# A two-head kernel rewritten: folded filter, three real products, taps on TensorE, transposing loads, one written-out order

## The chip, the cores and the metric

The kernel runs on one core of a Trainium2 chip. The core has a matrix engine (TensorE, PE in the profile, with its weight loads as PEld), a vector engine (VectorE, DVE), a scalar engine (ScalarE, ACT), a general engine (GpSimd, POOL) and a queue engine (SyncE, SP); the engines run side by side, each through its own instructions in order, and wait for one another by semaphores. DMA transfers are issued from the queues of SP, ACT and POOL. The time is the device time of one execution in microseconds.

## The reference

Two independent heads work on 2048 positions of 576 channels, in bf16, and their outputs stand side by side.

```python
def _A_ref(x, wqkv, wo):                     # H = 32 heads of 18 channels, W = 8 taps, dil = 2
    qkv = (x @ wqkv) ...                     # q, k, v
    idx = pos[:, None] - off[None, :]        # positions s, s-2, ..., s-14
    logits = jnp.einsum("bhsd,bhswd->bhsw", q, kg) * scale
    attn = _softmax(jnp.where(mask, logits, -1e9))
    o = jnp.einsum("bhsw,bhswd->bhsd", attn, vg)
    return o... @ wo

def _B_ref(q, k, v, shift_k, ssm_k, ssm_D):
    k_shift = sum over t < 4 of k_pad[:, t:t+S] * shift_k[:, 3-t]
    kv = k_shift * v
    y = irfft(rfft(kv, padded) * rfft(ssm_k, padded))[:S]     # a causal convolution of length 2048
    y = y + kv * ssm_D
    return q * y
```

Head A is an attention in which each position sees eight earlier positions two apart. Head B multiplies a short filter of k with v, convolves the product with a long filter per channel, adds a skip term and gates with q.

## The kernel before

Positions are cut into four blocks of 512 (`NBL`, `BL`), and head A also into two halves of 1024 (`hh`, `jj`).

Head B. The loads of k and v bring positions onto the partitions. `taps` (L412) forms the four-tap filter and the product with v on VectorE: per block four multiplications (L417), three additions (L420) and one multiplication by v (L421), each of 2304 elements. `mirror` (L423) turns half a block around on TensorE (L430) and adds and subtracts it by DMA, so that a transform of 256 rows per sign is enough for the data. `filter_spectrum` (L457) multiplies each block of 512 filter taps, loaded by transposing DMA into `kTok`, with cosine and sine tables `TK`: per block eight units of four pairs of matmuls (`mm3`, L454 and L455, 384 and 192 columns), each evicted by ScalarE (L466) into `Ks`. `turn_filter` (L474) adds neighbouring blocks of the filter's spectra by six DMAs on POOL's queue, three links of two. `x_spectrum` (L513) does the same for the data into `xw`, two pairs of matmuls a unit. `products` (L753) multiplies a data spectrum with a filter spectrum as complex numbers, four real products of 768 elements in one VectorE instruction (L757), 30 of them; `sums` (L764) adds them in PSUM with identity matrices in 64 x 64 tiles (L777); `inverse` (L789) goes back to positions (L799, L802), mirrors (`back`, L810), and the inner `gate` multiplies with q (L820) and stores.

Head A. x is partly turned on TensorE (L356, L370), partly loaded by transposing DMA (`turn_x`, L163). `project` (L276) makes q, k and v, with the 64 last rows of the contraction paired in two row groups (L297). `logits` (L541) multiplies q with shifted k on VectorE (L550) and sums over the channels of a head on TensorE (L559). `softmax` (L568) runs on VectorE and ScalarE. `spread` (L619) copies attention weights over partitions by DMA (L626), `weigh` (L638) multiplies them with v (L648) and adds over the eight taps in PSUM (L664, L675), and `output` (L696) multiplies with `wo` (L702, L705) and stores.

The order: VectorE's work is written in a fixed sequence. TensorE's units that can be moved (projections, spectra, inverses, outputs) stand in a list `units`; `until` (L252) takes a number of them, written out in `PLACES`, between the fixed steps. PSUM is two pools of two double banks. SP carries most loads, in the order in which the program issues them.

Of the kernel before, what the change touches and what calls it, by code (L numbers as in the profile page):

```python
# [18 lines left out]
PLACES = (  # L19
    11, 10, 11, 15, 1, 1, 2, 1, 1, 3, 0, 3, 2, 0, 3, 5, 2, 0, 4, 3, 4, 2, 1, 3, 1, 0, 6, 1, 7, 4, 4, 4, 2, 5,  # L20
    3, 2, 3, 0, 1, 2, 1, 2, 0, 1, 0, 2, 1, 0, 0, 0, 1, 2, 0, 1, 0, 1, 1, 2, 0, 1, 2, 3, 0, 0, 2, 1,
)


def view(t, offset, dims):

    return bass.AP(tensor=t.tensor, offset=t.offset + offset, ap=[list(t.ap[0])] + [list(d) for d in dims])
# [3 lines left out]
def kernel(  # L31
# [24 lines left out]

    PAD = 16
    KW = PAD + S
    KWH = PAD + 1024

    NBL, BL = 4, 512


    GORD = [0, 2, 1, 3]
    HD = 288
    SPB = 2 * 4 * D
    TH = 192

    ctx.enter_context(tc.manual_schedule())
    main = ctx.enter_context(tc.tile_pool(name="main", bufs=1))
    pp = ctx.enter_context(tc.tile_pool(name="pp", bufs=2, space=PSUM))

    def bank2(name, tag):
        return pp.tile([128, 2, 512], FP32, name=name, tag=tag)

    XW = 2 * SPB
    xw = main.tile([128, 4 * SPB], BF16, name="xw")  # L90
    TK = main.tile([128, 4, 2, BL], BF16, name="TK", tag="tabk")
    TX = main.tile([128, 2, 2, BL], BF16, name="TX", tag="tabx")
    TI = main.tile([128, 4, 2, 256], BF16, name="TI")

    def xT(kb, t0, n):
        return view(xw, XW + SPB * (t0 // 1024) + 1024 * kb + t0 % 1024, [[1, n]])

    def x5(jj):
        return view(xw, XW + SPB * jj + 4096, [[1, 512]])

    def wq(kb, comp, c0, n):
        return view(xw, comp * 5 * D + kb * D + c0, [[1, n]])


    wv = view(xw, 0, [[5 * D, 3], [D, 5], [1, D]])

    def load_w(eng, comp, to=None):
        to = wv[:, comp] if to is None else to
        eng.dma_start(to[:, 0:4, :], A_wqkv[0:512, comp * D:(comp + 1) * D].rearrange("(kb p) a -> p kb a", p=128))
        for r in range(2):  # L110
            eng.dma_start(to[64 * r:64 * r + 64, 4, :], A_wqkv[512:576, comp * D:(comp + 1) * D])

    s1 = ExitStack()
    sp1 = s1.enter_context(tc.tile_pool(name="s1", bufs=1, reuse_waits="tile"))
    pib = main.tile([128, 1], FP32, name="pib")
    nc.vector.memset(pib[:], float(np.float32(np.pi)))
    onesb = main.tile([1, 128], BF16, name="onesb")
    nc.vector.memset(onesb[:], 1.0)
    warm = sp1.tile([128, 1], FP32, name="warm")
    nc.scalar.activation(warm[:], pib[:], ACT.Sin)  # L120
    skrow = sp1.tile([1, 4 * D], BF16, name="skrow", tag="wraw")
    nc.sync.dma_start(skrow[:], B_shift_k.rearrange("d j -> (d j)").unsqueeze(0))

    Ks = main.tile([128, NBL, 2, 3, 4, TH], BF16, name="Ks")
    xnat = view(Ks, 0, [[4 * D, 4], [D, 4], [1, D]])
    n_all = view(Ks, 16 * D, [[1, 16 * D]]).bitcast(I32).rearrange("p (n f) -> p n f", n=9)
    krs = [view(Ks, 2 * D * i, [[D, 2], [1, D]]) for i in range(NBL)]
    kTok = main.tile([128, NBL, 4, D], BF16, name="kTok", tag="r_ktok")
    kjs, vts = [], []

    def load_x(qtr):
        nc.sync.dma_start(xnat[:, qtr], xf[512 * qtr:512 * qtr + 512, :].rearrange("(sb p) c -> p sb c", p=128))

    load_x(0)
    load_x(1)

    def load_k(i):

        eng = nc.sync
        kj = sp1.tile([128, 7, D], BF16, name="kj", bufs=2)  # L140
        r0 = BL * i
        if i == 0:
            nc.vector.memset(kj[0:1, 0:3, :], 0.0)
            eng.dma_start(kj[:, 3:7, :], kf[0:BL, :].rearrange("(p c) d -> p c d", c=4))
            for p0, p1 in ((1, 113), (113, 128)):
                eng.dma_start(kj[p0:p1, 0:3, :], bass.AP(tensor=kf.tensor, offset=kf.offset + (4 * p0 - 3) * D,
                                                         ap=[[4 * D, p1 - p0], [D, 3], [1, D]]))
        else:
            eng.dma_start(kj[:], bass.AP(tensor=kf.tensor, offset=kf.offset + (r0 - 3) * D,
                                         ap=[[4 * D, 128], [D, 7], [1, D]]))  # L150
        kjs.append(kj)

    def load_v(i):
        vt = sp1.tile([128, 4, D], BF16, name="vt", bufs=2)
        nc.sync.dma_start(vt[:], vf[BL * i:BL * i + BL, :].rearrange("(p c) d -> p c d", c=4))
        vts.append(vt)

    def load_filter(m):

        nc.sync.dma_start_transpose(kTok[:, m, :, :], B_ssm_k[:, BL * m:BL * m + BL])  # L160

    load_w(nc.sync, 0)
    def turn_x(h):  # L163

        r0 = 1024 + 512 * h
        nc.sync.dma_start(xnat[:, 2 + h, :, 512:576], xf[r0:r0 + 512, 512:576].rearrange("(sb p) c -> p sb c", p=128))
        nc.sync.dma_start_transpose(view(xw, XW + SPB + 512 * h, [[1024, 4], [1, 512]]), xf[r0:r0 + 512, 0:512])

# [312 lines left out]
    for i in range(NBL):  # L481
# [19 lines left out]
        if i == 2:  # L501
            load_filter(3)
# [396 lines left out]
```

## Time and profile before

| | |
|---|---|
| median of 3 runs | 238.58 us (237.65 to 240.54) |
| span of the profiled execution | 239.0 us |
| granted TensorE clock, mean | 0.984 |
| instructions | 4802 |
| bytes moved by DMA | 33.75 MB in 29559 packets |

The span of the profiled execution agrees with the median of the runs within 0.2%. In the rows of the profile, "L757" is a line of the kernel; "out<-in" names what an instruction writes and reads; after the bar stand the busy time of the group, the mean duration of one in ns, and the idle time of its engine just before. A matmul's duration includes the time until its results are out, so matmuls that follow one another overlap, and the distance between starts is the price of one in a row of them.

### The profile page before, as it was taken

To read this page: it belongs to the slowest core of one execution; us is meant where nothing else is said; L and a number is where in the kernel's file an instruction comes from. 1 tells how busy PE (TensorE), PEld (TensorE's weight loads), DVE (VectorE), ACT (ScalarE), POOL (GpSimd) and SP (SyncE) were. 2 spreads that over 40 slices of the span, in tenths; PEclk is the share of its full clock that TensorE was granted. 3 is DMA by queue.
4 is the path that set the end of the run, shared out by engine and by line. 5 is a ranking of instruction groups with operands and counts; after the bars stand their busy time and mean duration, and the time that the engine had idled before them with its cause. 6 is when DMAs were issued, how large, how long until landed. Compare 5 with 4: busy or idle time off the path is not lost.

```text
span 239.0 us, 4802 instructions
## 1 busy us (share of the span) xinstructions
PE 219.5 (92%) x2032; PEld 116.5 (49%) x2041; DVE 206.0 (86%) x152; ACT 156.7 (66%) x213; POOL 28.9 (12%) x61
## 2 busy tenths in 40 slices
PE   4899998999899999999998976989999999999991
PEld 2533443345545566533343443445555666666550
DVE  7599999999898896989899593889997899999931
ACT  6796778579965568565585575454568766736551
POOL 8600010202120000402108100000000000000000
PEclk9999999999999999999999999799999999999996
DMA  6999999999541000299975999907203102323233
GB/s 198 309 224 326 247 289 148 352 154 199 105 81 22 0 0 3 38 164 225 188 137 99 129 265 251 265 21 247 76 27 101 51 3 101 99 101 101 99 103 99
DMA packets 29559, 33.75 MB, mean 141 GB/s; under 512 B 16577, under 2 KB 23617, under 8 KB 29537
## 3 DMA queue, kind: packets, MB, share of 16 engines
q1 hardware_dynamic: 23712, 22.08, 38.0%
q0 software_dynamic: 3648, 9.00, 19.1%
q10 hardware_dynamic: 2176, 2.36, 2.9%
q8 instruction: 16, 0.26, 0.5%
q14 instruction: 7, 0.05, 0.1%
HBM read 13.11 MB, written 4.72 MB: 75 GB/s over the span
## 4 chain that ended last, share of the span: by engine, by line
PE 58%; DVE 21%; ACT 9%; SPq 5%; DMA 3%; issue 2%; DVEq 0%
PE ps_z L777 9%; PE ps_fk L454 8%; PE ps_wo L702 7%; PE ps_inv L799 7%; PE ps_proj L284 6%; SPq L626 5%; PE ps_log L559 4%; PE ps_fk L455 4%; DVE ab L420 3%; DVE tB L417 3%; PE ps_acc L664 3%; DMA X<-attn 3%; PE ps_acc L675 2%; DVE qk L648 2%; PE ps_back L810 2%
## 5 line engine op out<-in xcount | busy, mean ns | idle before, releaser
L757 DVE TENSOR_TENSOR qk<-xw,Ks 128x3072 bf16<-128x3072 bf16 x30 | 50.7, 1752 | 2.2 <-PE ps_z L777 2.0
L284 PE MATMUL ps_proj<-xw 128*128 128x512 bf16 x183 | 47.4, 385 | 2.2 <-ACT v L306 1.0
L550 DVE TENSOR_TENSOR prod<-qk 128x4096 bf16<-128x4096 bf16 (+1 forms) x20 | 40.6, 2074 | 4.3 <-PE ps_log L559 3.9
L454 PE MATMUL ps_fk<-kTok,TK 128*128 128x384 bf16 x128 | 32.6, 327 | 0.4 <-ACT qk L306 0.2
L455 PE MATMUL ps_fk<-kTok,TK 128*128 128x192 bf16 x128 | 31.4, 246 | 0.0
L284 PEld LDWEIGHTS <-xw 128*128 128x128 bf16 x192 | 17.1, 99 | 23.4 <-issue 8.6
L466 ACT ACTIVATE Ks<-ps_fk 128x576 bf16<-128x576 f32 x32 | 20.6, 651 | 12.0 <-PE ps_fk L455 11.9
L518 ACT ACTIVATE xw<-ps_fx 128x576 bf16<-128x576 f32 x32 | 19.9, 649 | 7.5 <-PE ps_fx L455 7.3
L306 ACT ACTIVATE qk<-ps_proj 128x1024 bf16<-128x1024 f32 x18 | 18.6, 1035 | 8.7 <-PE ps_proj L297 8.5
L784 ACT ACTIVATE Yall<-ps_z 128x768 bf16<-128x768 f32 x24 | 18.1, 810 | 4.4 <-PE ps_z L777 4.4
L454 PE MATMUL ps_fx<-ab,TX 128*128 128x384 bf16 x64 | 18.2, 332 | 1.8 <-ACT xw L518 1.7
L799 PE MATMUL ps_inv<-Yall,TI 128*128 128x288 bf16 (+2 forms) x128 | 19.0, 287 | 0.6 <-ACT yA L811 0.6
L702 PE MATMUL ps_wo<-qk,pv 128*128 128x288 bf16 x128 | 18.4, 287 | 0.6 <-ACT xw L518 0.6
L454 PEld LDWEIGHTS <-TK 128*128 128x128 bf16 x128 | 12.5, 98 | 12.4 <-issue 5.0
L803 ACT ACTIVATE yA<-ps_inv 128x576 bf16<-128x576 f32 (+2 forms) x16 | 10.4, 652 | 10.9 <-PE ps_inv L802 7.1
L777 PE MATMUL ps_z<-qk,ident 64*64 64x384 bf16 x288 | 16.7, 326 | 0.0
L420 DVE TENSOR_TENSOR ab<-ab,tB 128x2304 bf16<-128x2304 bf16 x12 | 16.3, 1358 | 0.4
L417 DVE TENSOR_TENSOR tB<-kj,skb 128x2304 bf16<-128x2304 bf16 x12 | 16.3, 1356 | 0.3
L648 DVE TENSOR_TENSOR P<-X,v 128x4096 bf16<-128x4096 bf16 x6 | 13.6, 2288 | 2.7 <-DMA X<-attn 1.2
L664 PE MATMUL ps_acc<-P,ident 64*64 64x512 bf16 x192 | 15.7, 379 | 0.3 <-DVE P L648 0.3
L455 PE MATMUL ps_fx<-ab,TX 128*128 128x192 bf16 x64 | 15.8, 247 | 0.0
L799 PEld LDWEIGHTS <-TI 128*128 128x128 bf16 x128 | 11.4, 98 | 6.8 <-issue 3.8
(126 smaller groups left out, 349.0 us busy)
## 6 DMA issues: line engine op xcount, KB each, us to landing
Ks<-Ks POOLq DMA_DIRECT2D x6, 576.0 KB, 11.5
qk<-attn SPq DMA_DIRECT2D x12, 256.0 KB, 7.0
kj<-in_B_k_dram SPq DMA_DIRECT2D x3, 1008.0 KB, 6.4
vt<-in_B_v_dram SPq DMA_DIRECT2D x4, 576.0 KB, 6.0
qB<-in_B_q_dram POOLq DMA_DIRECT2D x4, 576.0 KB, 4.1
out_dram<-qk ACTq DMA_DIRECT2D x8, 288.0 KB, 2.4
X<-attn SPq DMA_DIRECT2D x8, 256.0 KB, 9.4
out_dram<-qB SPq DMA_DIRECT2D x3, 576.0 KB, 4.8
```

The source lines that it names most:

```text
L284: nc.tensor.matmul(ps[:, jp, :], wq(kb, comp, 128 * ct, 128), xT(kb, 1024 * jj + 512 * jp, 512), start=(kb == 0), stop=False)
L417: dve(2304, lambda: nc.vector.tensor_tensor(o, kj[:, 3 - j:7 - j, :], skb[:, j, :].unsqueeze(1).to_broadcast([128, 4, D]), ALU.mult))
L420: dve(2304, lambda: nc.vector.tensor_tensor(kv, kv, o, ALU.add))
L454: nc.tensor.matmul(o[:, 0:2, :], w, rhs[:, 0:2, :], start=start, stop=stop)
L455: nc.tensor.matmul(o[:, 2, :], w, rhs[:, 2, :], start=start, stop=stop)
L466: nc.scalar.activation(Ks[:, 3 - m, cs, :, gi, :], acc3(ps), ACT.Copy, scale=(CSG, SSG)[cs][m] * 2.0 / 1024.0)
L550: r = dve(1024 * nj, lambda: nc.vector.tensor_tensor(view(prod, 0, [[256 * nj, 4], [256, nj], [1, 256]]), view(t, o + 256 * hh, [[0, 4], [ ...
L664: nc.tensor.matmul(acc[64 * o:64 * o + 64, h, :], ident[64 * h:64 * h + 64, 64 * h:64 * h + 64], view(P, 256 * u, [[2048, 2], [1, 256]])[6 ...
L702: nc.tensor.matmul(ps[:, r, 0:HD], oT(hh, j + 2 * r, t)[:, o:o + 128], wo[:, t // 2, t % 2, HD * h:HD * h + HD], start=(t == 0), stop=False)
L757: r = dve(3072, lambda: nc.vector.tensor_tensor(pr, view(xw, i * SPB + 4 * TH * t, [[4 * D, 2], [0, 2], [1, 4 * TH]]), view(Ks, (3 - j + i ...
L777: nc.tensor.matmul(acc[r][o:o + 64, h, 0:2 * TH], w[64 * h:64 * h + 64, 64 * h:64 * h + 64], pr[64 * h:64 * h + 64, part, cs, 2 * TH * s:2 ...
L799: nc.tensor.matmul(ps[:, c, 0:n], TI[:, sl, pm, 128 * c:128 * c + 128], Yall[:, j % 2, pm, sl, c0:c0 + n], start=(sl == 0), stop=(pm == 0 ...
```

## The change

The program is rewritten; most functions have new bodies. What differs:

- **Order.** All steps are first put into a list of 685 operations by name; a string `ORDER` then says in which order they are emitted and which PSUM slot (one of four double banks, or a pair of two) an operation takes. `PLACES` and its bookkeeping go. All SBUF buffers but some small ones are regions of one tile `mem`.
- **Loads.** Three quarters of x, all of k and v and all of the filter come through transposing DMA on SP's queue, so that channels lie on the partitions; the second quarter of x is loaded plainly (`xn`) and turned on TensorE (`nx0` to `nx2`). The weights are issued from ACT's queue. k and v are loaded in two parts of 1024 positions (`k0`, `va0`, `vb0`, ...; `k1`, ...), the second into the same buffers after the first. In the queue, the order is x, then parts of k, v and the filter mixed: `xt0 x0 x2 hl1 xt2 kt0 va0 hl0 vat0 k0 xt3 x3 hu1 hm0 hl3 vb0 hu0 vbt0 hl2 hu2 hu3`, then `vbt1 vat1 k1 hm1 vb1 ho1 kt1 va1`.
- **Taps.** The four-tap filter is done on TensorE, with diagonal matrices of `shift_k` in 64 x 64 tiles; VectorE multiplies the result in PSUM with v, the lower half of each block read backwards. `fold` turns and folds the product with matmuls against `[I | -I]` and `[I | I]`.
- **Filter.** Each block of 512 taps is folded at its middle tap into an even and an odd part of 256, by DMA: the lower half goes to a scratch in DRAM, is copied there in reverse order (`hm0`, `hm1`) and added by accumulating DMAs. Spectra take two pairs of matmuls a unit instead of four. They are written over the memory of x and the weights, so they start after the v projections. `turn_filter` adds neighbouring blocks with 18 DMAs of a third each.
- **Products.** A complex product is three real ones: besides the two parts of a spectrum their sum (`S`) or difference (`W`) is kept, one VectorE instruction each per block, and `products` multiplies three planes for one or two blocks at a time (2304 or 4608 elements). `sums` adds them with 32 x 32 tiles at all 16 places of the array.
- **Attention sums.** `weigh` adds four channel groups in one unit, also in 32 x 32 tiles. The projection of v picks strided columns of the weights and writes 64 columns per matmul; the tail of the contraction is padded with zeros to a fifth full block.
- **Inverse and gates.** The inverse works on thirds of 192 channels. The sum and the difference of its two parts are taken on VectorE. For three blocks the lower half of the output is left in mirrored order, gated with a mirrored q (`qm`, a copy in DRAM), stored to a scratch (`y0l` to `y2l`) and copied in reverse order to the output (`y0m` to `y2m`); for the last block TensorE flips it.

VectorE's order from the first logits on is: logits of the first half, taps of the first half of k and v mixed with the first softmax, logits of the second half, second softmax mixed with the second taps, the 18 products of `weigh`, the sums `W` and `S`, the products `z` with the gates. TensorE's order begins (names: `p` component, channel tile, half; `L` logit sums; `t` taps; `f` fold; `k` filter spectra; `x` data spectra; `a` attention sums; `Z` sums; `i` inverse; `o` output):

```
nx1 nx0 nx2 p000 p010 p110 p100 p120 p020 L000 L001 p130 p030 L010 L011 p200 L012 L002 p140 p040 L003
p240 p141 p111 p121 p001 L013 L014 L004 t00 t01 t04 p210 p230 t03 t02 p101 p011 f000 p021 p031 L110 f010
L100 f011 p131 L111 L101 p041 p201 L102 p241 p211 L112 L103 p231 L113 f001 k200 L104 L114 k220 p221 k100
k300 f02 t14 t10 t11 f12 ...
```

The core of the diff (added lines; `mm`, `act`, `tt` are matmul, activation and tensor_tensor, `M` and `M1` views of `mem`):

```diff
+def emit(op, slot, PS):
+    if op.take:
+        a, b = (slot, slot + 1) if op.take == 1 else PAIRS[slot]
+        op.box.ps, op.box.step = PS[:, 2 * a:2 * a + 2], 1024 * (b - a)
+    op.fn()
...
+    VS, US = AB - 18432, AB - 9216
...
+    def load_x(qtr):
+        xbar(f"x{qtr}", M(XT + 512 * qtr, [[2048, 4], [1, 512]]), xf[512 * qtr:512 * qtr + 512, 0:512])
+        xbar(f"xt{qtr}", M1(X4 + 512 * qtr, 512), xf[512 * qtr:512 * qtr + 512, 448:576])
+
+    def load_k(pr):
+        c0, r0, r1 = (PAD, 0, 1024) if pr == 0 else (0, 1008, 2048)
+        xbar(f"k{pr}", M(KT + c0, [[1040, 4], [1, r1 - r0]]), kf[r0:r1, 0:512])
+        xbar(f"kt{pr}", M1(KT + 4 * 1040 + c0, r1 - r0), kf[r0:r1, 448:576])
...
+    def taps(pr):
...
+            def unit(box=box, jobs=jobs):
+                for l in range(4):
+                    for w, h, ab, c, bank in jobs:
+                        mm(box.ps[64 * c:64 * c + 64, bank, :], dg(w, h, l), kt(w, h, ab, l), start=(l == 0),
+                           stop=(l == 3), tile_position=(64 * h, 64 * c))
...
+            for lo in range(2):
+                s = [[512, nb], [1 - 2 * lo, 256]]
+                b = 255 if lo else 256
+                op(f"t{pr}{n}{'hl'[lo]}", lambda box=box, s=s, b=b, lo=lo, n=n, nb=nb: tt(
+                    M(KV + 1024 * n + 256 * lo, [[512, nb], [1, 256]]), view(box.ps, b, s), M(VT + 1024 * n + b, s),
+                    ALU.mult), box, free=bool(lo))
...
+                dma(f"hm{d // 2}", low_rows(scm, (d - 1) * 256, [[256 * D, 2], [D, 255], [1, D]]),
+                    low_rows(scr, (d - 1) * 256 + 255, [[256 * D, 2], [-D, 255], [1, D]]))
...
+    def filter_spectrum(m, cs, gi):
...
+            for c in range(2):
+                mm3(box.ps, M1(TK + 1024 * c + 512 * cs + 128 * gi, 128), thirds((HO if cs else HU) + 2 * D * m + D * c),
+                    c == 0, c == 1)
...
+    def turn_filter(m):
+        for t in range(3):
+            for cs, (x, y) in enumerate(((US, VS), (VS, US))):
+                dma(f"turn{m}{cs}{t}", M1(x + SPB * (3 - m) + 768 * t, 768), M1(y + SPB * (4 - m) + 768 * t, 768),
+                    nc.gpsimd, accum_op=ALU.add)
...
+                for u in range(W):
+                    for s in range(4):
+                        for i in range(4):
+                            o = i ^ s
+                            mm(view(box.ps[32 * o:32 * o + 32], box.step * (i // 2) + 512 * (i % 2), [[1, 512]]), I32S[1][32 * i:32 * i + 32],
+                               M(Ps[s] + 256 * u, [[2048, 2], [1, 256]])[32 * i:32 * i + 32],
+                               start=(u == 0), stop=(u == W - 1), tile_position=(32 * i, 32 * o))
...
+        op(f"z{j}{t}{i}", lambda: tt(
+            M(pr, [[2304, n], [768, 3], [1, 768]]), M(BS + i * SPB + o, [[SPB, n], [PL, 3], [1, 768]]),
+            M(VS + (3 - j + i) * SPB + o, [[SPB, n], [PL, 3], [1, 768]]), ALU.mult))
...
+            for k, (src, st, n, o, w) in enumerate(terms):
+                for g in range(4):
+                    for r in range(4):
+                        c = r ^ g
+                        mm(view(box.ps[32 * c:32 * c + 32], box.step * (r // 2) + 512 * (r % 2) + o, [[TH, n], [1, TH]]),
+                           I32S[w][32 * r:32 * r + 32], M(pr + src + TH * g, [[st, n], [1, TH]])[32 * r:32 * r + 32],
+                           start=(i == 0 and k == 0), stop=(i == j and k == len(terms) - 1),
+                           tile_position=(32 * r, 32 * c))
...
+        op(f"g{j}h", lambda: tt(M1(y + 2304, 1152), M1(y, 1152), M1(y + 1152, 1152), ALU.subtract))
+        op(f"g{j}l", lambda: tt(M1(y, 1152), M1(y, 1152), M1(y + 1152, 1152), ALU.add))
+        g = M(qb, [[1152, 2], [1, 1152]])
+        op(f"g{j}g", lambda: tt(g, M(y, [[2304, 2], [1, 1152]]), g, ALU.mult))
...
+        dma(f"y{j}m", rows(outf, (BL * j + 255) * 2 * D + D, [[HD, 2], [-2 * D, 256], [1, HD]]),
+            rows(scy[:], o, [[HD, 2], [D, 256], [1, HD]]))
```

More of the change, by code (lines that the diff above doesn't have):

```diff
@@ L1 @@
-from collections import deque
 from contextlib import ExitStack
-from functools import partial
 import numpy as np
@@ L105 @@
[L105 to L125, printed above, removed]
```

1245 lines of the change are left out of this document (610 added, 635 removed).

## The prediction

> **What bounds the kernel now.** I read the first part of the page, then the busy time by stretches of 12 us, then the groups by line with the shapes apart, then the timeline of TensorE and of the DMA queues for the price of single steps.
>
> ```profile
> PE 219.5 (92%) x2032; PEld 116.5 (49%) x2041; DVE 206.0 (86%) x152; ACT 156.7 (66%) x213; POOL 28.9 (12%) x61
> PE 58%; DVE 21%; ACT 9%; SPq 5%; DMA 3%; issue 2%; DVEq 0%
> ...
> 0.00:12.00 12.00, 7.95 (x48) 4.68 (x49) 7.51 (x18) 8.67 (x13) 8.66 (x35) 1.00 0.83 254
> 144.00:156.00 12.00, 9.30 (x73) 4.55 (x72) 7.98 (x4) 5.79 (x10) 0.00 (x0) 0.86 0.98 249
> 192.00:204.00 12.00, 12.00 (x170) 8.04 (x166) 11.88 (x8) 7.83 (x12) 0.00 (x0) 1.00 0.15 51
> 228.00:239.00 11.00, 5.28 (x76) 3.50 (x74) 1.88 (x3) 4.39 (x7) 0.00 (x0) 0.81 0.33 109
> ```
>
> Two engines fill the span together. The first line gives TensorE 92% and VectorE 86%; the chain of waits (second line) runs over TensorE for 58% and VectorE for 21%. In the stretch rows (busy us of TensorE, weight loads, VectorE, ScalarE, GpSimd, then granted clock, DMA share, GB/s) both are full at 192 to 204 us, and both are half empty only in the first and last 12 us and, waiting for DMA, around 150. So a gain must come off both, and neither alone is worth its full size. The span is 239.0 us, the median of the three runs 238.58 (237.65 to 240.54), so I add nothing around a span.
>
> **VectorE, row by row.**
>
> ```profile
> L757 DVE TENSOR_TENSOR qk<-xw,Ks 128x3072 bf16<-128x3072 bf16 x30 | 50.7, 1752 | 2.2 <-PE ps_z L777 2.0
> L550 DVE TENSOR_TENSOR prod<-qk 128x4096 bf16<-128x4096 bf16 x16 | 36.0, 2288 | 4.1 <-PE ps_log L559 3.9
> L420 DVE TENSOR_TENSOR ab<-ab,tB 128x2304 bf16<-128x2304 bf16 x12 | 16.3, 1358 | 0.4
> L417 DVE TENSOR_TENSOR tB<-kj,skb 128x2304 bf16<-128x2304 bf16 x12 | 16.3, 1356 | 0.3
> L550 DVE TENSOR_TENSOR prod<-qk 128x2048 bf16<-128x2048 bf16 x4 | 4.9, 1220 | 0.2 <-ACT Ks L466 0.2
> L421 DVE TENSOR_TENSOR ab<-ab,vt 128x2304 bf16<-128x2304 bf16 x4 | 5.4, 1358 | 0.1
> L417 DVE TENSOR_TENSOR ab<-kj,skb 128x2304 bf16<-128x2304 bf16 x4 | 5.4, 1352 | 0.0
> L820 DVE TENSOR_TENSOR qB<-yA,qB 128x2304 bf16<-128x2304 bf16 x3 | 4.1, 1351 | 0.0
> L358 DVE COPY xw<-ps_x 128x512 bf16<-128x512 bf16 x4 | 1.7, 425 | 3.3 <-PE ps_x L356 3.3
> L588 DVE TENSOR_TENSOR attn<-attn 128x256 f32<-128x256 bf16 x1 | 0.4, 427 | 0.0
> ```
>
> Removed: the four taps and the gate by v, 16.3 + 16.3 + 5.4 + 5.4 = 43.4 us, all of it on VectorE's path at the start; the 30 products, 50.7 us; the gates at the end, about 5.7 (4.1 in the row, 1.6 in the shorter ones of the last block). Two sine tables fewer and smaller copies take about 4 more.
>
> Added: 20 multiplications that read the taps from PSUM (16 of 512 elements, 4 of 256). No row is one; 512 elements cost 0.43 us in L358 and 256 fp32 elements cost 0.43 in L588, so 0.43 to 0.85 each; I take 0.6, nearer the middle because one operand is fp32 and one bf16: 11 us (8 to 15). Eight sums `W` and `S` of 2304 elements as L420: 8 x 1.358 = 10.9. The new products: six of 2304 (1.36 each) and twelve of 4608, which the line through 3072 at 1752 ns and 4096 at 2288 ns puts at 2.56: 8.1 + 30.7 = 38.8. So three products for four save 50.7 - 38.8 - 10.9 = 1.0 us, nearly nothing. New gates: for three blocks two of 1152 (0.77 by the line through 3072 and 2304) and one of 2304, for the last nine of 384 (about 0.38): 8.7 + 3.4 = 12.1, 6.4 more than before, since the mirroring back moves from TensorE to here. VectorE's sum: 206.0 - 43.4 - 50.7 - 5.7 - 4 + 11 + 10.9 + 38.8 + 12.1 = 175, or 31 less.
>
> **TensorE, start to start.**
>
> ```profile
> 23.71 1.90 PE L284 MATMUL ps_proj<-xw 128*128 128x512 bf16 x8
> 58.19 0.33 PE L454 MATMUL ps_fk<-kTok,TK 128*128 128x384 bf16 x1
> ...
> 58.44 0.33 PE L454 MATMUL ps_fk<-kTok,TK 128*128 128x384 bf16 x1
> 164.06 1.15 PE L702 MATMUL ps_wo<-qk,pv 128*128 128x288 bf16 x8
> 171.17 1.92 PE L664 MATMUL ps_acc<-P,ident 64*64 64x512 bf16 x32
> 225.87 0.33 PE L777 MATMUL ps_z<-qk,ident 64*64 64x384 bf16 x4
> 226.03 0.49 PE L777 MATMUL ps_z<-qk,identn 64*64 64x384 bf16 x8
> 230.93 0.82 PE L799 MATMUL ps_inv<-Yall,TI 128*128 128x192 bf16 x8
> 25.86 0.64 PE L346 MATMUL ps_ti<-ident,TX 128*64 128x128 bf16 x16
> ```
>
> Eight full matmuls of 512 columns take 1.90 us, less one's tail about 0.216 apart. A filter pair (384 + 192 columns) starts 0.245 us after the one before (58.19, 58.44). 288 columns: 0.123. 192 columns with new weights each: 8 in 0.82, or 0.082. Four 64 x 64 matmuls of `ps_z` take 0.33 together, as long as the single one of 384 columns at 58.19: they run four abreast, and eight take one slot of 0.16 more; 32 of `ps_acc` take 1.92, eight slots of 0.216.
>
> Filter spectra: 132 pairs become 64, -68 x 0.245 = -16.7. Sums over products: 120 slots of 0.163 become, sixteen 32 x 32 matmuls abreast, 48 of 0.163 and 24 of 0.082: -9.8. Accumulators of attention: 64 slots become 32: -6.9. Inverse: the added `A` and the mirroring (L802, L810: 48 matmuls, about 6 us) go, six come: -5. Flips and transposes of x: -3. Projections: 243 slots become 270, as the tail of the contraction is padded rather than paired: +5.8. Taps: 40 slots of 0.216: +8.6; folding: 72 matmuls of 256 columns at 0.11: +7.9. Output projection: +2. Together -17, all on the path where TensorE is full. That 16 run abreast no row shows. The bounds are 0.16 a group (no loss against four abreast) and four slots, 0.65; I take the first, because the four in 0.33 start a few ns apart, each with its own weights, so sixteen start within one slot.
>
> [...]
>
> **Loads and queues.** All of x but one quarter, k, v and the filter come through transposing loads on SP's queue, and nothing overtakes there.
>
> ```profile
> L167 SPq DMA_TRANSPOSE xw<-in_A_x_dram x2: 5058/5354/5651, 10.6 to 17.2; - x2
> DMA to landing us min/median/max: 7.1/8.0/9.0
> ...
> L160 SPq DMA_TRANSPOSE kTok<-in_B_ssm_k_dram x4: 3462/5488/14702, 23.6 to 53.6; - x4
> Ks<-Ks POOLq DMA_DIRECT2D x6, 576.0 KB, 11.5
> X<-attn SPq DMA_DIRECT2D x8, 256.0 KB, 9.4
> out_dram<-qk ACTq DMA_DIRECT2D x8, 288.0 KB, 2.4
> out_dram<-qB SPq DMA_DIRECT2D x3, 576.0 KB, 4.8
> ```
>
> A unit of 512 x 512 occupies SP for 5.06 to 5.65 us between other loads (L167); the cheapest of L160, 1.125 units, 3.46, or 3.1 a unit. The change has 18.3 units where before had 6.5: 57 to 103 us of SP. I take 4 (73 us), because the plain loads that shared the queue with L167 are mostly gone. Order in the queue: 8.6 units up to `x3`, 2.1 more to `vb0` (a mirroring copy `hm0` between), then 7.5 to `va1`. At 4 us: `x3` lands near 40, `vb0` near 50, `va1` near 85.
>
> **The path.** Start: `x0` issues near 2 and lands 7 later; three projections of ten slots and an eviction of 1.0 follow, slow at first, as the seven before took:
>
> ```profile
> 11.11 2.83 PE L284 MATMUL ps_proj<-xw 128*128 128x512 bf16 x7
> L306 ACT ACTIVATE qk<-ps_proj 128x1024 bf16<-128x1024 f32 x18 | 18.6, 1035 | 8.7 <-PE ps_proj L297 8.5
> L559 PE MATMUL ps_log<-prod,E 128*32 128x512 bf16 x160 | 11.6, 383 | 1.2 <-ACT ab L434 0.8 <-DVE prod L550 0.4
> 16.35 1.35 DVE ab L417
> 230.06 1.51 ACT Yall L784 x2
> 231.57 0.71 ACT yA L811
> 234.91 0.56 DVE qB L820
> ```
>
> 0.40 each instead of 0.216, so +1.4 (the eviction: L306). First logits product at 19 to 20, against 16.35 for VectorE's first steady work before. Logits of the first half: 8 x 2.29 + 2 x 1.22 = 20.8, to 40. Then VectorE waits: before `t00` TensorE has, in the order written out, 9 projections of 2.16, 4 of 1.08, 3 more of 2.16 and ten logit sums of about 0.45 (L559: eight matmuls, two slots), 34.8 us from 11 on, the slow start and the turning of x with it some 3 more, so 49: 9 us idle, and `x3` and `vb0` are just there. Taps and softmax of the first half, 12 us, to 61. Logits of the second and the rest of softmax, 22, to 83. Last logit sums behind projections, 3.5; `k200` stands ahead of them in TensorE's order and needs the folded filter by way of SP and GpSimd, 2 more (0 to 10); softmax and taps again, 13: 101.5. Eighteen weighted products as L550, 41.2, and 3 for the spread copies (9.4 to land): 146. GpSimd's turning of the spectra is three links of 11.5 = 35 from about 118, so 153, just ahead of `W1`; each us more is a us of the time. Up to `z000` the eight sums (10.9) and a wait for the last data spectra (5): 162. Products 38.8 with the gates that lie among them, about 6.5: 207; TensorE has 38 us of work there. Tail: last sums 0.7, eviction 1.5 as the pair at 230.06, inverse 1.3, eviction 0.8, two gates and a flip 1.2, store 2.4: 8, giving **215 us**. The last 9 us of before (230.06 to 239.0) are the same chain, so the tail neither gains nor loses.
>
> **The rivals.** (a) Transposing loads stay at L167's loaded price, 5.35 a unit: `vb0` lands at 62 instead of 49, all behind it slips by 13: 228. L160's median speaks for it, its minimum against it. At 7.4 a unit the time would pass 243.
>
> (b) Small tiles run only four abreast: sums +29, accumulators +21; between 162 and 207 TensorE then has 67 us of work for 45, of which some can be moved: about +14 there and a few before: 231. For it: the 28 ns spacing of L346 (16 in 0.64 us). Against: those run two abreast at 128 columns, which alone needs 27 ns.
>
> (c) Slower: the mirroring copies (`hm0`, `hm1`, `qm`, `y0m` to `y2m`) have an outermost dimension of 2 or 3, and if only so many of the 16 DMA engines carry them, 288 KB that take 2.4 us on all take 19 on two. `hm0` (574 KB, up to 38) stands in SP's queue ahead of `vb0`, so VectorE and TensorE wait there up to 33 us, and `y2m`, issued about 6 us after the last product, ends some 17 after the last store would: 265. It turns slower than before when a copy of 576 KB takes over some 22 us. The rows cannot say; no large copy of before has such a dimension. [...]
>
> **The numbers.** Forecast 0.57; (a) 0.13; (b) 0.10; (c) 0.20, of which 0.06 with only the last copy late (about 232). Two per cent, about what a measurement can tell from no change, is 233.8 to 243.4. Faster: 0.56 of the forecast's, 0.09 of (a), 0.07 of (b) and 0.04 of the mild (c) = 0.76; within: 0.01 + 0.02 + 0.03 + 0.02 = 0.08; slower: 0.14 of (c) and 0.02 of (a) = 0.16. Below, the waits of 2, 3, 5 and 2 us may vanish and the taps cost 8: 203. Above, (a), (b) and the mild (c) reach 238; what lies beyond is (c) in full.
>
> **What would show it.** Right: VectorE near 175 us busy, first product at 19 to 21, a hole before the first tap product of about 9 us, sixteen `Z` matmuls in one slot, both engines near full from 50 on. Wrong: transposing loads above 7 us a unit, VectorE waiting for `vb0` or for the turning copies, a copy of the mirror still running when the last gate ends.

## The result: 358.0 us, and the profile after

| | before | after |
|---|---|---|
| median | 238.73 us (237.65 to 240.54, 4 runs) | 358.01 us (352.60 to 361.49, 4 runs) |
| ratio, 95% interval | | 1.481 (1.466 to 1.496) |
| span of the profiled execution | 239.0 us | 358.2 us |
| VectorE / TensorE busy | 206.0 / 219.5 us | 172.8 / 199.8 us |
| granted TensorE clock, mean | 0.984 | 0.841 |

The change is slower by 119 us; the prediction was 215 us and its range ended at 238. The ratio is taken from the fast runs alone, for the kernel after those of 352.60 and 356.05 us, while the profile is of the run of 359.98 us. The first part of the page and the chain of waits after, to hold against the first two lines that the prediction shows:

```profile
PE 199.8 (56%) x3134; PEld 128.6 (36%) x3134; DVE 172.8 (48%) x138; ACT 148.0 (41%) x180; POOL 88.0 (25%) x112
PE 29%; DMA 22%; issue 18%; SPq 11%; POOL 8%; ACT 6%; DVE 3%; ACTq 0%; DVEq 0%; POOLq 0%
```

Both engines lost the work that they were to lose (forecast 175 and about 202), but neither is busy for more than 56% of the span. The chain no longer runs over them: DMA, `issue` (an engine stood and the profile shows nothing that it waited for), SP's queue and GpSimd hold 59% of it, TensorE and VectorE 32%. The time went into holes. Busy time by stretches of the kernel after (columns: TensorE, weight loads, VectorE, ScalarE, GpSimd, granted clock, DMA share, GB/s):

```profile
0.00:34.00 34.00, 11.72 (x53) 5.92 (x54) 6.87 (x15) 11.81 (x13) 20.81 (x55) 1.00 1.04 210
107.00:176.00 69.00, 0.66 (x7) 0.35 (x4) 0.96 (x1) 1.23 (x2) 18.89 (x4) 0.53 0.42 49
217.00:248.00 31.00, 6.24 (x40) 4.25 (x41) 2.54 (x3) 3.99 (x8) 2.54 (x3) 0.56 0.42 68
289.00:348.00 59.00, 46.73 (x1497) 35.93 (x1471) 49.77 (x37) 34.80 (x35) 0.00 (x0) 1.00 0.31 95
```

Two holes of 69 and about 29 us have hardly any work on TensorE and VectorE, and the granted clock is 0.53 and 0.56 there, beside 1.00 in the two other stretches; the mean of 0.841 follows from the holes (it is 0.943 in the run without the accumulating copies, below) and does not cause them. Who waited for whom (engine and line, releaser, us in total, times, longest):

```profile
ACT mem L561 <- PE PS L505: 103.7, 7, 69.0
DVE mem L426 <- ACT mem L413: 73.6, 1, 73.6
...
PE PS L504 <- issue: 68.9, 1, 68.9
...
PE PS L504 <- DMA mem<-scm: 33.1, 2, 29.7
...
DVE mem L639 <- PE PS L504: 28.5, 1, 28.5
...
PE PS L362 <- ACT mem L292: 17.4, 1, 17.4
```

L504 and L505 are the two matmuls of a filter spectrum. TensorE stands 68.9 us before the first of them (`k200`). The logit sums stand behind it in TensorE's order, ScalarE evicts them late, and so the second softmax (L426) waits 73.6 us. The second hole is the same again at a later spectrum; VectorE's weighted product (L639) loses 28.5 us to it. What came before is in the chain between 84 and 250 us (start, us, what):

```profile
84.50 16.34 DMA scm<-scr
...
101.13 10.76 POOL mem L186 x4
111.89 32.08 issue
143.97 14.01 POOL mem L186 x2
157.98 18.72 issue
176.72 9.58 DMA mem<-scm
...
202.50 39.22 DMA mem<-scm
```

`scm` is the scratch with the filter's lower half in reverse order: `hm1` fills it until 100.84, and then GpSimd issues the accumulating copies `mem<-scm` that add it to the even and odd parts. It stands for 32.08 and 18.72 us between them, and the last ones are 9.58 and 39.22 us on the way. The same copies among the DMA issues (count, KB each, median us from issue to landing):

```profile
mem<-scm POOLq DMA_DIRECT2D x4, 288.0 KB, 11.1
scm<-scr SPq DMA_DIRECT2D x2, 573.8 KB
mem<-scm POOLq DMA_DIRECT2D x4, 285.8 KB, 37.6
```

Eight copies do the same thing on nearly the same number of bytes. The four with 288.0 KB go to 128 partitions; the four with 285.8 KB go to 127 (in `fold_filter`, `p0` is 1 for `c == 0`, as partition 0 holds the middle tap). One partition less, and the landing takes 3.4 times as long.

### The profile page after: what moved, and what is told of

The parts are those of the page before. It is cut to its first block, busy times and chain, and to the rows that moved or that the text cites. A ratio compares the mean times of both kernels' runs of the same rounds, so it can differ in the third digit from the quotient of the medians.

```text
span 358.2 us, 7069 instructions
## 1 busy us (share of the span) xinstructions
PE 199.8 (56%) x3134; PEld 128.6 (36%) x3134; DVE 172.8 (48%) x138; ACT 148.0 (41%) x180; POOL 88.0 (25%) x112
## 4 chain that ended last, share of the span: by engine, by line
PE 29%; DMA 22%; issue 18%; SPq 11%; POOL 8%; ACT 6%; DVE 3%; ACTq 0%; DVEq 0%; POOLq 0%
DMA mem<-scm 14%; SPq L189 11%; POOL mem L186 8%; PE PS L694 6%; PE PS L362 6%; DMA scm<-scr 5%; PE PS L783 4%; PE PS L504 4%; PE PS L757 4%; ACT mem L764 3%; PE PS L505 2%; PE PS L654 2%; DMA mem<-in_B_k_dram 2%; DMA mem<-mem 1%; DMA mem<-in_B_v_dram 1%
## 5 line engine op out<-in xcount | busy, mean ns | idle before, releaser
L504 PE MATMUL PS<-mem 128*128 128x384 bf16 x128 | 35.5, 342 | 102.0 <-issue 68.9
L362 PE MATMUL PS<-mem 128*128 128x512 bf16 (+1 forms) x320 | 58.3, 402 | 22.5 <-ACT mem L292 17.4
L561 ACT ACTIVATE mem<-PS 128x576 bf16<-128x576 f32 x32 | 18.9, 664 | 103.9 <-PE PS L505 103.7
L639 DVE TENSOR_TENSOR mem<-mem 128x4096 bf16<-128x4096 bf16 x18 | 40.1, 2285 | 34.2 <-PE PS L504 28.5
L399 DVE TENSOR_TENSOR mem<-mem 128x4096 bf16<-128x4096 bf16 (+1 forms) x20 | 40.3, 2071 | 28.6 <-ACT mem L366 20.7
L504 PEld LDWEIGHTS <-mem 128*128 128x128 bf16 x128 | 13.0, 101 | 110.1 <-issue 72.6
L362 PEld LDWEIGHTS <-mem 128*128 128x128 bf16 (+1 forms) x320 | 32.5, 148 | 46.6 <-issue 28.7
L186 POOL DMA_DIRECT2D mem<-scm x8 | 33.0, 5277 | 62.2 <-issue 51.3
L742 DVE TENSOR_TENSOR mem<-mem 128x4608 bf16<-128x4608 bf16 (+1 forms) x18 | 37.9, 2152 | 2.9 <-PE PS L757 2.9
L426 DVE TENSOR_TENSOR mem<-mem 128x1024 bf16<-128x1024 bf16 x2 | 1.4, 692 | 73.6 <-ACT mem L413 73.6
L505 PE MATMUL PS<-mem 128*128 128x192 bf16 x128 | 32.6, 255 | 0.0
L466 DVE TENSOR_TENSOR mem<-PS,mem 128x512 bf16<-128x512 f32 (+1 forms) x20 | 11.7, 629 | 18.7 <-DMA mem<-in_B_v_dram 9.1
L764 ACT ACTIVATE mem<-PS 128x1536 bf16<-128x1536 f32 x12 | 17.3, 1449 | 7.4 <-PE PS L757 7.4
L582 ACT ACTIVATE mem<-PS 128x576 bf16<-128x576 f32 x32 | 19.1, 663 | 2.3 <-PE PS L505 2.2
L783 PE MATMUL PS<-mem 128*128 128x192 bf16 x192 | 17.3, 246 | 3.6 <-ACT mem L764 3.6
L783 PEld LDWEIGHTS <-mem 128*128 128x128 bf16 x192 | 15.9, 98 | 5.2 <-issue 4.9
L694 PEld LDWEIGHTS <-mem 128*128 128x128 bf16 x160 | 15.8, 101 | 5.2 <-issue 0.7
## 6 DMA issues: line engine op xcount, KB each, us to landing
mem<-in_B_q_dram SPq DMA_DIRECT2D x5, 288.0 KB, 3.0
scr<-mem POOLq DMA_DIRECT2D x4, 288.0 KB, 3.5
mem<-scm POOLq DMA_DIRECT2D x4, 288.0 KB, 11.1
```

The costliest lines, as they stand in the source:

```text
L186: op(name, lambda: (eng or nc.sync).dma_start(o, i, **kw))
L362: mm(box.ps[p, jp, :], w, xT(kb, 1024 * hh + 512 * jp, 512), start=(kb == 0), stop=(kb == 4), tile_position=(0, 64 * a))
L399: op(f"l{hh}{ug}{ct}", lambda prod=prod, nt=nt, qo=qo, ko=ko, ug=ug: tt(M(prod, [[nt, 4], [1, nt]]), M(qo, [[0, 4], [1, nt]]), M(ko + 2 + ...
L504: mm(view(ps, 0, [[320, 2], [1, TH]]), w, rhs[:, 0:2, :], start=start, stop=stop)
L505: mm(view(ps, 640, [[1, TH]]), w, rhs[:, 2, :], start=start, stop=stop)
L639: op(f"w{n}{ct}", lambda: tt(M(P, [[2048, 2], [256, W], [1, 256]]), M(XB[n], [[2048, 2], [256, W], [1, 256]]), M(vo + 2, [[256, 2], [2, W] ...
```

## The experiments

Theory F: the copies over 127 partitions run on one of the 16 DMA engines, and the mirroring copies, with an outermost 2, on two; cut so that more engines carry them, they land sooner. In the kernel after, the packets of SP's queue took 13.4% of the 16 engines' time from 55 to 60 us, with `hm0` on the way, and 13.1% from 88 to 94, with `hm1`; two of 16 are 12.5%. For 127 partitions the figure stands below. Against it: A, accumulating copies from the scratch are slow as such; L, the transposing loads fill the DMA engines. Later: Q, what remains is a matter of places in the queues of SP and GpSimd; C, the DMA engines are full in the first 110 us, so that moving one transfer pushes another. Runs of one kernel lie up to 13 us apart here (352.6 to 361.5; 275.1 to 288.4 below), so I read nothing into smaller differences between single runs. Where no other time of the kernel before is given, it took 241.61 us on the same chip.

**Only the copies over 127 partitions cut in two** (112 and 15):

```diff
-                p0, row = (1, 0) if c == 0 else (0, 127)
-                dma(f"h{nm}{b}{c}", M(t + 2 * D * ds[0] + D * c, [[2 * D, 2], [1, D]])[p0:128], ...
+                    for p0, p1, row in ((1, 113, 0), (113, 128, 112)) if c == 0 else ((0, 128, 127),):
+                        nc.gpsimd.dma_start(M(t + 2 * D * ds[0] + D * c, [[2 * D, 2], [1, D]])[p0:p1], ...
```

> The four accumulating copies that add the mirrored half of the filter on partitions 1 to 127 are each cut into 112 and 15 partitions; nothing else. Theory F (a copy over 127 partitions is carried by one DMA engine, 254 packets at about 93 ns one after the other): these copies land in about 11 us, as their neighbours over 128 partitions did, instead of 38; TensorE's waits of 69 and 29 us for the first filter spectra shrink to under 20 and under 5; span 262 to 285. Theory A (an accumulating copy in GpSimd's queue is slow however many engines carry it): landings stay near 38 us, span 350 to 362. Theory L (the transposing loads fill the DMA engines, the copies only queue behind them): the same as A, 350 to 362.

Measured: 279.4 us, in F's range, 70 us under those of A and L. Its DMA issues:

```profile
mem<-scm POOLq DMA_DIRECT2D x4, 288.0 KB, 13.6
...
mem<-scm POOLq DMA_DIRECT2D x4, 252.0 KB, 18.8
...
mem<-scm POOLq DMA_DIRECT2D x4, 33.8 KB, 18.1
```

Their medians are 13.6 to 18.8 us (F had said about 11), and between two of them GpSimd stands 5.6 us at most. The same kernel timed in three rounds:

> The kernel with only the 127-partition copies cut in 112 and 15, again, timed in three rounds for an interval: 274 to 284 us by theory F, a ratio of 1.15 to 1.19 to the kernel before; theory A would have it at 350 to 362.

Measured: 282.65 us (275.10 to 288.39, 4 runs) beside 238.63 of the kernel before, a ratio of 1.18. So these four lines are 75 of the 119 us (78 between the fastest runs of the two kernels, 352.60 and 275.10). TensorE's larger wait for the folded filter (L504) is still 17.4 us (18.9 in the first run of this kernel), the smaller is gone.

**The count of partitions by itself, in the kernel before.** Its six accumulating copies `Ks<-Ks` go from SBUF to SBUF, 128 partitions each, and touch no scratch; two run side by side in each of three links.

```diff
-        for m in (3, 2, 1):
+        for m, cuts in ((3, (127, 126)), (2, (125, 120)), (1, (113, 112))):
             for cs in range(2):
-                nc.gpsimd.dma_start(Ks[:, 3 - m, cs], Ks[:, 4 - m, 1 - cs], accum_op=ALU.add, max_dma_last_dim=2304)
+                for p0, p1 in ((0, cuts[cs]), (cuts[cs], 128)):
+                    nc.gpsimd.dma_start(Ks[p0:p1, 3 - m, cs], Ks[p0:p1, 4 - m, 1 - cs], ...
```

> The kernel before, in which each of its six accumulating copies that turn the filter's spectra (128 partitions, 576 KB, 11.5 us) is cut in two by partitions: 127+1, 126+2, 125+3, 120+8, 113+15, 112+16. [...] Rival A (accumulating copies that start at a shifted row are slow, the number of partitions does not matter): all six parts land in 11 to 15 us and the time stays at 238 to 246.

Measured: 329.8 us, 88 more than the kernel before beside it. By size (127 partitions are 571.5 KB, 126 are 567.0, 125, 120, 113 and 112 follow), then by stretches:

```profile
Ks<-Ks POOLq DMA_DIRECT2D x1, 571.5 KB, 73.7
Ks<-Ks POOLq DMA_DIRECT2D x1, 567.0 KB, 69.8
Ks<-Ks POOLq DMA_DIRECT2D x1, 562.5 KB, 14.4
Ks<-Ks POOLq DMA_DIRECT2D x1, 540.0 KB, 15.5
Ks<-Ks POOLq DMA_DIRECT2D x1, 508.5 KB, 51.1
Ks<-Ks POOLq DMA_DIRECT2D x1, 504.0 KB, 49.8
```

```profile
160.00:172.00 12.00, 0.00 (x0) 0.00 (x0) 0.00 (x0) 0.00 (x0) 0.00 (x0) 0.50 0.07 14
215.00:240.00 25.00, 0.00 (x0) 0.00 (x0) 0.00 (x0) 0.00 (x0) 0.00 (x0) 0.50 0.07 13
```

The two links with 127 and with 113 partitions take 50 to 74 us, the one without such a number 15. What runs beside or behind the slow copy lands with it (126 and 112 partitions in 69.8 and 49.8 us, and even pieces of 4.5 and 72 KB in 70.2 and 49.8), so only the link as a whole is a measurement. The stretch rows show why: nothing computes, and the DMA share is 0.07 at 13 to 14 GB/s. One engine of 16 is 0.0625. F, with one engine for 127 and for 113 partitions, had put their landings at 28 to 50 us, which was too low, and the kernel at 260 to 330, where it is; A had put it at 238 to 246. The copies over 125 and 120 partitions landed in 14.4 and 15.5 us; on how many engines, no row shows. What is shown is that the links with 127 and with 113 kept about one engine busy. The kernel after shows the same in its first hole, while a copy over 127 partitions from DRAM is on the way:

```profile
126.00:142.00 16.00, 0.00 (x0) 0.00 (x0) 0.00 (x0) 0.00 (x0) 0.00 (x0) 0.50 0.08 12
```

In these 16 us the trace has 172 packets, one every 93 ns.

**The mirroring copies `hm0` and `hm1` in eight pieces**, 127 partitions left as they are:

```diff
-                dma(f"hm{d // 2}", low_rows(scm, (d - 1) * 256, [[256 * D, 2], [D, 255], [1, D]]), ...
+                    for e in (d - 1, d):
+                        nc.sync.dma_start(low_rows(scm, e * 256, [[72, 8], [D, 255], [1, 72]]),
+                                          low_rows(scr, e * 256 + 255, [[72, 8], [-D, 255], [1, 72]]))
```

> The two mirroring copies within DRAM (hm0, hm1) are issued as two copies each with an outermost dimension of 8 (pieces of 144 bytes) instead of one with an outermost dimension of 2; nothing else. Theory F: each lands in 5 to 9 us instead of 13 and 16, vb0 lands some 6 earlier, the first tap product starts at 62 to 66 instead of 69, and the accumulations start at 85 to 93 instead of 101; their own landing time stays; span 338 to 350. Theory A: the copies matter little, 350 to 362. Theory L: SP stands 13 us behind hm0 because of the loads, and this stays; 350 to 362.

Measured: 343.4 us, in F's range and 9 us under the fastest run of the kernel after. SP stands 10.1 and 11.2 us over each mirroring copy and the load behind it, in place of 13.9 and 16.1, and the first tap product comes at 65.0 (69.4). So the shape that rival (c) named costs something, about a tenth of the matter; on how many engines the eight pieces ran, no row shows.

**The start by another order on ScalarE's queue** (`const0` first, `w1` behind the turning of x, `w2` and `shift_k` behind the first projection, the exponential's table later):

> Only the written order changes: on ACT's queue the loads of w1, w2 and the short filter are issued after the evictions of the turned x, and the exponential's table is asked for just before the first softmax. Theory F with a late start of its own (TensorE's first projection waited until 24.6 us for ACT, which stood in its queue of loads): first projection at 10 to 15 us, first logits product at 22 to 27 instead of 34.7; but the filter's chain sets the later waits, so the span falls by 3 to 12 only, 346 to 355. Rival (the first projection waits for the transposing load of x, not for ACT): first product stays at 33 to 36, span 354 to 362.

Measured: 361.0 us, the rival's range. ScalarE's loads, and then SP's, in the same stretch:

```profile
12.84 7.46 ACTq L187 DMA_DIRECT2D mem<-in_A_wqkv_dram  x2
...
25.33 9.17 ACTq L187 DMA_DIRECT2D sh<-in_B_shift_k_dram  x2
```

```profile
14.11 1.26 SPq L190 DMA_TRANSPOSE mem<-in_A_x_dram  x1
15.42 2.38 SPq L190 DMA_TRANSPOSE mem<-in_B_k_dram  x1
17.84 2.85 SPq L190 DMA_TRANSPOSE mem<-in_B_v_dram  x1
...
23.43 7.02 SPq L190 DMA_TRANSPOSE mem<-in_B_k_dram  x1
30.50 3.37 SPq L190 DMA_TRANSPOSE mem<-in_A_x_dram  x2
```

Two pairs of issues hold ScalarE's queue for 7.5 and 9.2 us, while SP is issuing transposing loads, and its evictions stand behind them. In the kernel after it is the same: four weights take the queue from 1.29 to 13.53, SP's first three loads take theirs from 0.81 to 12.78. The issue was moved and met the next transposing load; the first logits product came at 38.7, later than either theory had it.

**All of it together** (cut copies, eight pieces for the filter, q and output mirrorings, that start):

> All three together, and the mirrored q and the mirrored outputs also in 8 pieces. Theory F: the two long waits nearly go, the start is 10 us earlier, the tail ends 3 to 6 us sooner; span 228 to 255. Theories A and L: 335 to 355, the two long waits stay.

Measured: 277.7 us, a miss: no better than the cut copies alone. The first logits product is at 40.1 (33.8 with the cut alone), the wait ahead of the first filter spectrum is still 11.7 us, and the three copies for q hold SP for 10.5 us. What was won at one place was lost at another.

**The filter's steps moved forward in the queues**, with cut copies and eight pieces (SP: `vb0 vbt0 hl3 hl2 hm0 hm1` behind `x3`, ahead of the upper halves and of `k1`; GpSimd: `hs0 hs1` behind `hl0`, `hs2 hs3` ahead of the tail pads):

> The changed kernel with the 127-partition copies cut into 112 and 15, the mirroring copies of the filter in eight pieces, and the filter's steps moved forward in the queues of SP and GpSimd (lower halves stored right after they land, the second pair loaded and both mirroring copies issued ahead of the upper halves and of the second half of k). Theory Q (what is left of the wait ahead of the first filter spectrum, 19 us in the kernel with cut copies alone, is the place of the second mirroring copy in SP's queue, behind the second half of k): the wait falls under 5 us and the time to 252 to 264. Rival B (the accumulating copies as such take that time, wherever they stand): the wait stays at 12 to 20 us and the time at 268 to 280.

Measured: 269.4 us. TensorE waits only 1.3 us for the folded filter, as Q says, but the time is in B's range: the first tap product, at 68.4 with the cut alone, now comes at 75.4. The timelines of SP, and the waits, of this kernel:

```profile
43.04 14.30 SPq L531 DMA_DIRECT2D scm<-scr  x4
```

```profile
ACT mem L541 <- DMA mem<-in_B_ssm_k_dram: 10.2, 1, 10.2
```

The mirroring copies hold SP for 14.30 us, the upper halves come behind them, and ScalarE waits 10.2 us to negate one (L541), with evictions behind it.

**The start by GpSimd's queue**, with cut copies:

```diff
-    load_w(0, nc.scalar)
+    load_w(0, nc.gpsimd)
...
```

> The changed kernel with the 127-partition copies cut, and the start altered: weights and shift_k issued from GpSimd's queue in place of ScalarE's, the third quarter of x loaded after the first half of k, the exponential's table loaded after the sines. Theory H (a plain copy issued on ScalarE's queue stands until the transposing loads that SP is issuing are through, 12.2 us for four weights beside 12.0 us of SP, and ScalarE's evictions stand behind it): first logits product at 21 to 26 in place of 34, time 266 to 272. Rival I (the weights themselves take until then to arrive, or the transposed x does): first product at 31 to 36, time 275 to 282.

Measured: the first logits product at 25.6, as H says, and 283.6 us, above both ranges and no gain against 282.65. The first tap product stays at 67.4 (VectorE waits 14.4 us for `vb0`, which stands behind `hm0` in SP's queue), and the wait for the folded filter becomes 20.9 us. The early start was worth nothing here, because later waits had dates of their own.

**Both:**

> The steps of the two other kernels together (cut copies, mirroring in eight pieces for filter, q and the output, filter's steps forward, weights on GpSimd's queue). If both theories Q and H hold, the gains add up and the time is 236 to 250, with VectorE waiting less than 40 us between the first product and the last gate. If either falls, 256 to 278.

Measured: 276.7 us; the gains do not add up. `hs2` and `hs3` now stand in GpSimd's queue ahead of the tail pads of k while their load has not landed (GpSimd waits 10.4 us for it, until 57), and VectorE stands 19.4 us for those pads ahead of its last products of the first logits (`l014`).

**All queues written anew** (weights at the head of GpSimd's queue, k, v and x of the first half ahead of the filter's second pair, and four more places):

> The changed kernel with the cut copies, the filter's mirroring and the three output mirrorings in eight pieces, weights on GpSimd's queue at its head, and a new order in the queues: SP brings all of k, v and x of the first half ahead of the second pair of the filter, the mirroring copies come behind those, GpSimd stores the lower halves early but behind the diagonals and takes the second pair after the tail pads of k, ScalarE negates the filter after the first logits, and a row copy stands behind the spread copies. If only queue places are left of the lateness (theory Q), the first product is at 22 to 26, the first tap product at 56 to 66, no wait over 4 us stands ahead of the first filter spectrum, and the time is 238 to 254. Rival C (the DMA engines carry as much as they can in the first 110 us, so each transfer moved forward pushes another back): the first tap product stays at 66 to 76 and the time at 258 to 275.

Measured (the kernel before 238.01 beside it): 272.0 us, first tap product at 67.2: rival C's ranges. SP and TensorE:

```profile
0.81 7.09 SPq L190 DMA_TRANSPOSE mem<-in_A_x_dram  x2
7.94 20.27 SPq L190 DMA_TRANSPOSE mem<-in_B_ssm_k_dram  x2
```

```profile
28.04 14.60 PE L363 MATMUL PS<-mem 128*128 128x512 bf16 x60 [20.91 <-DMA mem<-in_A_x_dram]
```

With the weights early on GpSimd's queue, two transposing loads that took 1.36 and 1.35 us of SP in the kernel after take 20.27, x arrives at 28, and the weights take 21.6 us to land (6.3 in the kernel after). The first projection is later than before the effort. A full set of DMA engines is a plausible reason: in this kernel their share is 0.9 or more from 13.5 to 27 us, at only 60 to 61 GB/s. What makes those loads that slow was not tried.

**The accumulating copies left out.** The convolution then uses the filter without its folded part.

```diff
-                dma(f"h{nm}{b}{c}", M(...)[p0:128], low_rows(scm, ...), nc.gpsimd, accum_op=ALU.add)
+                op(f"h{nm}{b}{c}", lambda: None)
```

> The changed kernel without the eight accumulating copies of the reversed lower half into the even and odd parts of the filter (so the convolution uses the wrong filter), nothing else altered. Theory F: both waits of TensorE for these copies (69 and 28.5 us) go, nothing else is late behind them, and the time is 252 to 268. Rival (the next in line, the turning of the spectra or the spread copies, takes their place): one wait of over 15 us on those stands in the trace and the time is 275 to 310.

Measured: 263.6 us (the kernel before 238.01 beside it), as F says. The eight copies cost 358.0 - 263.6 = 94 us (89 to 98 over the runs of the kernel after); the two waits named above add up to 69 + 28.5 = 97.5. The longest wait that came up for the filter's spectra in their place is 10.3 us (VectorE's weighted product), under the rival's 15.

**The best order found**, timed in three rounds:

> The kernel with the filter's steps moved forward (269 us in one look), and three more places changed: the first upper part of the filter ahead of the mirroring copies, ScalarE's negations behind the first logits' evictions, the row copy behind the spread copies; the three output mirrorings in eight pieces. Theory Q: the first tap product comes at 66 to 71 (75.4 before), the wait for spread copies ahead of the fourth weighted product falls from 8 to under 4 us, the last 10 us after the last gate to under 8, and the time is 252 to 263. Rival C (DMA is full there, moving gives back elsewhere): 264 to 275. Neither theory puts it ahead of the kernel before.

Measured: 262.02 us (257.66 to 264.14, 4 runs) beside 238.63, a ratio of 1.10, and beside 282.65 for the cut alone: places in queues, with the eight pieces, are worth another 21 us (17 between the fastest runs, 275.10 and 257.66). The first tap product is at 64.5, the fourth weighted product waits 2.3 us, the tail after the last gate is 7 us. No version came under the kernel before.

```profile
PE 198.3 (76%) x3134; PEld 127.2 (49%) x3134; DVE 173.1 (67%) x138; ACT 144.9 (56%) x178; POOL 68.3 (26%) x116
```

## Why the prediction was wrong, step by step

Starts on VectorE's timeline, in us, with the forecast's path:

| step | forecast | after | best order |
|---|---|---|---|
| first logits product | 19.5 | 34.7 | 35.2 |
| first tap product | 49 | 69.4 | 64.5 |
| logits of the second half begin | 61 | 84.0 | 83.9 |
| they end | 83 | 108.0 | 108.8 |
| first weighted product | 101.5 | 198.4 | 127.9 |
| 17 of the 18 weighted products done | 144 | 273.2 | 174.5 |
| `z000` | 162 | 289.4 | 193.6 |
| end | 215 | 358.2 | 259.3 |

The eighteenth weighted product stands behind two of the sums in the order as written, so the row takes 2.3 us off the forecast's 146.

**The step that failed** is "`k200` stands ahead of them in TensorE's order and needs the folded filter by way of SP and GpSimd, 2 more (0 to 10)". It was 69 us. I had seen the place in TensorE's order and who waits behind it, but I priced eight accumulating copies with a number that no row carried, and never looked at their shapes. The second wait, 28.5 us, was not in the forecast at all: `ho00` stands in GpSimd's order behind the loads of `wo`, which wait for the softmax, and takes 39.22 us from 202.50. Leaving the copies out confirms both (94 us); cutting those over 127 partitions returns 75 to 78.

**Rival (c)** had the right mechanism and too small a reach. It named the copies with an outermost 2 or 3; the ones that decided have 127. That only so many engines carry a copy was a supposition there, with no row behind it. The traces show about one engine for accumulating copies over 127 and 113 partitions (a share of 0.07 to 0.08) and about two for `hm0` and `hm1` (13.1 to 13.4%); for 125 partitions they do not tell. For its own copies (c) was too dear: it put 574 KB on two engines at up to 38 us, and `hm1` landed in 16.34; the wait at the first tap product for `vb0` was 9.1 us, not 33, and eight pieces returned 9 to 18 us. So the 0.14 given to (c)'s slow form stood on the right mechanism and the wrong copies, and the range could not hold what was never priced.

**What held.** VectorE's sum (175; 172.8) and TensorE's (about 202; 199.8). Groups with the shapes apart:

```profile
L742 DVE TENSOR_TENSOR mem<-mem 128x4608 bf16<-128x4608 bf16 x12 | 30.3, 2552 | 2.6 <-PE PS L757 2.6
...
L466 DVE TENSOR_TENSOR mem<-PS,mem 128x512 bf16<-128x512 f32 x16 | 10.3, 682 | 9.5 <-DMA mem<-in_B_v_dram 9.1 <-PE PS L458 0.2
```

The products of 4608 elements take 2.552 us (2.56 forecast), those from PSUM 0.68, in the middle of 0.43 to 0.85. Sixteen tiles of 32 x 32 run abreast:

```profile
291.63 0.54 PE L757 MATMUL PS<-mem 32*32 32x384 bf16 x32
```

Thirty-two in 0.54 us, the last one's duration included, are two slots, and the first sixteen start within 0.05 us; rival (b) falls. Rival (a) falls as well: single loads cost SP from 2.4 us a unit (`k0`, 4.87 for two) to 5.3 (`x0`, `x2` and a tail, 11.97 for 2.25), but `x3` was issued by 32.4, where I had it land near 40. The loads came late only behind it. SP stood 15.9 us, until 48.46, because `hu1` is written over q of the first half and waited for a logits product, which the late start had moved; and the load behind `hm0` took 13.15. So `vb0` was issued at 63.78. That SP waits for VectorE there was not in my sum.

**What was mis-sized, without the copies.** The best order is still 44 us over the forecast. Of these 44, 16 are the start: I let projections run from 11, and TensorE waited until 24.6 because ScalarE, held by its own issues, did not evict the turned x (the row L362 <- L292 above). The first logits end 5 later still, where `l014` waits 4.9 us for the tail pads of k, but the hole of 9 that I had behind them takes that up, and the first tap product is again 16 late. Between it and the second logits 19 us stand for 12, and the second logits take 25 for 22. So the weighted products begin 26 us late; seventeen of them are done 31 late, and the sums end 32 late. Another 8 are products and gates: the row 289 to 348 has VectorE busy for 49.8 of 59 us; I counted 38.8 + 6.5 = 45 there, where the gates of my own sum alone are 12.1, so 5 are an error of addition; most of the rest I put down to evictions (L764) between sums and inverses, which no run isolates. The last 5 are behind the last gate, where 7 us stand for 2.4.

**GpSimd's turning**, three links from 118 on, was to end just ahead of `W1`; no run shows VectorE waiting for it. Behind the last gate I had a store of 2.4 us; the mirrored copy made it 9.9, and 7 in eight pieces.

**Smaller slips of the working.** By its own terms the low end of the range is 200 and not 203. The stretches that I called half empty at the start and around 150 have TensorE busy for 66% and 78%. And I added nothing around a span, where the runs that list both show a time 1.6 to 1.8 us above the span. None of these bears on the outcome.

## What to carry to other kernels

Before an accumulating copy goes on the path, write down how many partitions it covers: over 127 (all but one) or 113 it ran on about one DMA engine here (a share of 0.07 to 0.08), and cutting 127 into 112 and 15 costs one more issue. Which other counts lose engines, these runs do not settle. A price "0 to 10" for work of which the trace has no like is no bound; take the slowest that the shape allows, and see who stands behind the waiting unit in its engine's fixed order. And while one wait has a date of its own, gains ahead of it come out as a longer wait: remove the latest first, then look again.

## What the runs showed of the hardware

- An accumulating copy over 127 or 113 partitions used about one DMA engine of 16: a share of 0.07 at 13 to 14 GB/s from SBUF (127 and 113), and 0.08 at 12 GB/s from DRAM (127), a packet every 93 ns. GpSimd stood for 32.08 and 18.72 us between the issues of such copies; the profile shows nothing that it waited for.
- The mirroring copies from DRAM to DRAM, with an outermost 2, used about two: 13.4% of the 16 engines' time for `hm0` (55 to 60 us) and 13.1% for `hm1` (88 to 94 us).
- Plain loads on ScalarE's queue stood while SP issued transposing loads: 12.24 us for four beside 11.97 us of SP. The same loads from GpSimd's queue did not hold ScalarE (first logits product at 25.6 in place of 33.8 to 34.7).
- In one kernel two transposing loads took 20.27 us of SP beside weights loaded from GpSimd's queue, and the trace shows 60 to 61 GB/s from 13.5 to 27 us at a DMA share of 0.9 or more; the cause stays open.
- In the holes, where TensorE had hardly any work, the granted clock was 0.50 to 0.56; from 289 to 348 us, with TensorE busy for 47 of 59 us, it was 1.00.
